# One of five wq loads issued by an ordinary, row-per-partition `dma_start`

## The chip, the cores and the metric

The kernel runs on one core of one Trainium2 chip. The metric is device microseconds of that core, the median of several executions; lower is better. A "span" is the time of one profiled execution from its first to its last instruction; it is about 1.7 us shorter than the device time of the same run.

## The reference, cut to what matters

```python
# x (1,1,640); k_cache, v_cache (1,32,32768,192); wq (640, 32*192); wo (6144, 640); all bf16
h  = x + attention(layernorm(x)) @ wo     # q = layernorm(x) @ wq; keys and values: the last 4096 positions
h2 = h + gmlp(layernorm(h))               # w_in (640,1536), w_out (768,640)
```

One token is decoded. Nearly all the work is reading: wq is 7.9 MB, the window of keys and values of 32 heads 100.7 MB, wo 7.9 MB, the gMLP weights 2.9 MB. Nothing is read twice, so the kernel is a stream of loads with arithmetic behind it.

## The kernel before

All large loads are issued on SP (the sync engine's queue) by one helper that builds the DMA instruction itself:

```python
def load(out, in_):
    eng = nc.sync
    eng.add_instruction(mybir.InstDMACopy(
        name=nc.get_next_instruction_name(), mode="Copy", queue="qSPDynamicHW",
        ins=eng.lower_ap_dma(in_, for_custom_bir_dma=True),
        outs=eng.lower_ap_dma(out, for_custom_bir_dma=True)))
...
wq_v = A_wq.rearrange("(c p i) n -> c p (i n)", c=DC, i=4)   # 5 blocks; 32 source rows of 48 KB each
...
def dma_wq(i):
    t = kvp.tile([P, KVE], BF16, tag="kv", name="wq_t")
    for c in range(2 * i, min(2 * i + 2, DC)):
        load(t[:, (c % 2) * HD:(c % 2 + 1) * HD], wq_v[c])
    tiles[("wq", i)] = t
...
plan = [("kv", lambda i=i: dma_wq(i)) for i in range(NWQ)]   # wq comes first,
...                                                          # then k, v, wo, w_in, w_out in order of use
issue()                                                      # issues until the buffers are all taken
```

Source and destination of a wq load name the same 128 x 6144 elements in the same order, but the source is described as 32 rows of 24576 elements (four rows of wq run together), the destination as 128 partitions of 6144. Three tiny loads (x, and two scalars) go out by `nc.scalar.dma_start` on ACT. The program that is built from this carries a mark, "precooked", on those three and on no load of SP: an ordinary `dma_start` gets it where the shape allows, the hand-built instruction does not.

Of the kernel before, what the change touches and what calls it, by code (L numbers as in the profile page):

```python
# [16 lines left out]
def kernel(  # L17
# [14 lines left out]
    nc = tc.nc  # L32
    P = nc.NUM_PARTITIONS
# [6 lines left out]
    HD = H * Dh  # L40
# [15 lines left out]
# [6 lines that stand above are left out]
# [11 lines left out]
    wq_v = A_wq.rearrange("(c p i) n -> c p (i n)", c=DC, i=4)  # L73
# [27 lines left out]
    def dma_wq(i):  # L101
        t = kvp.tile([P, KVE], BF16, tag="kv", name="wq_t")
        for c in range(2 * i, min(2 * i + 2, DC)):
            load(t[:, (c % 2) * HD:(c % 2 + 1) * HD], wq_v[c])
        tiles[("wq", i)] = t

    def dma_pair(kind, cache, t_):
# [6 lines left out]
    def dma_wo(q):  # L114
# [7 lines left out]
        tiles[("wo", q)] = t  # L122

    plan = [("kv", lambda i=i: dma_wq(i)) for i in range(NWQ)]
    for t_ in range(2):
        plan.append(("kv", lambda t=t_: dma_pair("k", A_k_cache, t)))
# [531 lines left out]
```

## Time and profile before

| | before |
|---|---|
| device time | 286.6 us (286.29 to 286.65, 3 runs) |
| span of the profiled run | 284.7 us |
| bytes moved, mean rate | 119.53 MB, 420 GB/s |
| large queue's packets, share of 16 engines' span | 97.8% |
| first wq issue on SP | 551 ns, from 0.74 us |
| first packet of wq | 2.073 us |
| last landing of wo_t to the end of the span | 10.6 us |

These are lines of the page of the kernel before. The first two rows have one entry for each of 40 equal slices of the span: the busy share of the 16 DMA engines in tenths (9 is 90% or more), and the rate. The last row is the queue that SP's loads run on: packets, MB, share of 16 engines' span.

```profile
DMA  8999999999998999999999999999999999999993
GB/s 332 435 435 408 435 429 402 444 463 435 435 435 382 435 442 443 427 464 424 414 442 421 443 428 439 407 457 428 410 435 456 442 442 383 435 435 425 401 406 141
DMA packets 5404, 119.53 MB, mean 420 GB/s; under 512 B 973, under 2 KB 2254, under 8 KB 2830
...
q1 hardware_dynamic: 5384, 119.35, 97.8%
```

The engines are busy from the first slice to the last but one. A 48 KB packet takes 1.815 us, so 16 engines carry 16 x 49152 B / 1.815 us = 433 GB/s. The Trainium skill, "DMA: Bandwidth & Descriptors", section "Where 436 GB/s comes from", gives 435 GB/s as the ceiling of the fabric, and this trace agrees. (The same section says that for loads from HBM the HBM side, about 358 GB/s, binds; here, with one core running, it did not: the page has 119.34 MB of HBM reads, 419 GB/s over the span.) With the engines this full, what is left to win without moving fewer bytes is the start, before the engines run, and the tail, after the last load that the end waits for.

The next lines are from the timeline of the first 12 us (start, duration, engine and line, what, and in brackets the idle time before it). SPq and ACTq are the queues that issue DMAs; an issue's duration is the sequencer's work on it, not the transfer.

```profile
0.74 3.15 SPq L58 DMA_DIRECT2D wq_t<-in_A_wq_dram  x5
...
0.91 0.50 ACTq L155 DMA_DIRECT2D x_row<-in_A_x_dram  x1
...
2.21 0.28 PE L241 MATMUL sm_ps<-ones_bf,x_row 1*128 1x1 bf16 x5 [2.21 <-DMA x_row<-in_A_x_dram]
...
6.49 0.16 DVE L245 COPY x_pc<-sm_ps 128x5 f32<-128x5 f32 x1
...
7.36 1.90 SPq L58 DMA_DIRECT2D k_t<-in_A_k_cache_dram  x3
```

Five wq issues run one after another on SP. The single records behind the first line are 551, 568, 594, 632 and 615 ns. The first ends at 1.288 us and its first packet starts at 2.073 us, so 0.785 us pass between issue and data. The k_t issue at 7.36 us waits for the first wq load to land (they share a semaphore).

The view of the wq tile tells the same by issue (min/median/max, ns), and how long each load took from issue to landing; the chain of waits shows the last load on the path and the last computation (start, duration).

```profile
L58 SPq DMA_DIRECT2D wq_t<-in_A_wq_dram x5: 551/594/632, 0.7 to 3.3; - x5
...
DMA to landing us min/median/max: 6.6/11.2/15.7
```

```profile
260.22 13.82 DMA wo_t<-in_A_wo_dram
...
281.75 0.32 DVE o_sb L629
```

The last wo_t load lands at 260.22 + 13.82 = 274.04 us. Then come 10.6 us of short dependent steps; the gMLP weights, queued behind wo, land meanwhile, and their last packet ends at 280.95 us.

### The profile page before, as it was taken

To read this page: it belongs to the slowest core of one execution; us is meant where nothing else is said; L and a number is where in the kernel's file an instruction comes from. 1 tells how busy PE (TensorE), PEld (TensorE's weight loads), DVE (VectorE), ACT (ScalarE), POOL (GpSimd) and SP (SyncE) were. 2 spreads that over 40 slices of the span, in tenths; PEclk is the share of its full clock that TensorE was granted. 3 is DMA by queue.
4 is the path that set the end of the run, shared out by engine and by line. 5 is a ranking of instruction groups with operands and counts; after the bars stand their busy time and mean duration, and the time that the engine had idled before them with its cause. 6 is when DMAs were issued, how large, how long until landed. Compare 5 with 4: busy or idle time off the path is not lost.

```text
span 284.7 us, 3101 instructions
## 1 busy us (share of the span) xinstructions
PE 167.1 (59%) x1110; PEld 65.3 (23%) x1110; DVE 218.4 (77%) x288; ACT 75.2 (26%) x380; POOL 2.3 (1%) x10
## 2 busy tenths in 40 slices
PE   0329935773755377725852585536971767764774
PEld 0103412221211022211220121112320222321463
DVE  7300099889999999998499999996699949995443
ACT  2001247413274431122344440143101010202301
POOL 3000000000000000000000000000000000000000
PEclk9999979796598557955799558955797797999785
DMA  8999999999998999999999999999999999999993
GB/s 332 435 435 408 435 429 402 444 463 435 435 435 382 435 442 443 427 464 424 414 442 421 443 428 439 407 457 428 410 435 456 442 442 383 435 435 425 401 406 141
DMA packets 5404, 119.53 MB, mean 420 GB/s; under 512 B 973, under 2 KB 2254, under 8 KB 2830
## 3 DMA queue, kind: packets, MB, share of 16 engines
q1 hardware_dynamic: 5384, 119.35, 97.8%
q8 instruction: 8, 0.13, 0.2%
q14 instruction: 6, 0.05, 0.0%
q10 hardware_dynamic: 6, 0.00, 0.0%
HBM read 119.34 MB, written 0.00 MB: 419 GB/s over the span
## 4 chain that ended last, share of the span: by engine, by line
DMA 42%; DVE 41%; PE 13%; issue 2%; SPq 1%; ACT 0%; DVEq 0%; ACTq 0%
DVE k_t L316 22%; DMA k_t<-in_A_k_cache_dram 21%; DMA v_t<-in_A_v_cache_dram 9%; DMA wq_t<-in_A_wq_dram 7%; DMA wo_t<-in_A_wo_dram 5%; PE sc_ps L264 5%; DVE S L309 5%; DVE ob L437 4%; DVE S L330 4%; PE sc_ps L323 3%; PE pv_174 L412 1%; PE attn_ps L473 1%; SPq L58 1%; PE sm_ps L340 1%; DVE gm L342 1%
## 5 line engine op out<-in xcount | busy, mean ns | idle before, releaser
L316 DVE TENSOR_TENSOR k_t<-k_t,q_205 128x6144 bf16<-128x6144 bf16 x32 | 107.1, 3351 | 13.1 <-DMA k_t<-in_A_k_cache_dram 13.1
L323 PE MATMUL sc_ps<-k_t,ident_bf 128*128 128x512 bf16 x282 | 87.1, 468 | 50.6 <-DVE k_t L316 50.6
L306 ACT ACTIVATE k_t<-k_t 128x192 bf16<-128x192 bf16 x144 | 49.9, 347 | 32.8 <-DVE k_t L316 32.8
L323 PEld LDWEIGHTS <-ident_bf 128*128 128x128 bf16 x282 | 30.6, 113 | 98.3 <-issue 63.9
L306 ACT ACTIVATION_READ_ACCUMULATOR k_t<-k_t 128x1 f32 x144 | 26.8, 186 | 0.0
L309 DVE TENSOR_REDUCE S<-k_t 128x16 f32<-128x3072 bf16 x8 | 26.8, 3345 | 0.0
L264 PE MATMUL sc_ps<-wq_t,xn_126 128*128 128x512 bf16 x60 | 17.4, 449 | 10.4 <-DMA wq_t<-in_A_wq_dram 8.1
L330 DVE TENSOR_REDUCE S<-sc_ps 128x16 f32<-128x512 f32 (+1 forms) x32 | 21.8, 682 | 0.5 <-PE sc_ps L323 0.5
L273 DVE TENSOR_SCALAR sp_f<-sm_ps 128x1 f32<-128x1 f32 x3 | 0.3, 153 | 25.3 <-PE sm_ps L270 25.3
L359 ACT ACTIVATE E_125<-S,bias 128x64 bf16<-128x64 f32 x10 | 3.5, 360 | 48.1 <-DVE bias L349 48.1
L359 ACT ACTIVATE E_123<-S,bias 128x64 bf16<-128x64 f32 x12 | 4.2, 360 | 41.9 <-DVE bias L349 41.9
L359 ACT ACTIVATE E_124<-S,bias 128x64 bf16<-128x64 f32 x10 | 3.5, 361 | 37.9 <-DVE bias L349 37.9
L266 ACT ACTIVATE q_205<-sc_ps 128x512 bf16<-128x512 f32 x6 | 3.6, 597 | 30.1 <-PE sc_ps L264 30.1
L264 PEld LDWEIGHTS <-xn_126 128*128 128x128 bf16 x60 | 6.5, 109 | 20.9 <-issue 13.6
L412 PE MATMUL pv_174<-v_t,E_124 128*8 128x512 bf16 (+1 forms) x72 | 8.9, 521 | 2.0 <-DMA v_t<-in_A_v_cache_dram 2.0
L342 DVE TENSOR_REDUCE gm<-sm_ps 2x1 f32<-2x128 f32 x16 | 4.5, 278 | 7.1 <-PE sm_ps L340 7.1
L412 PE MATMUL pv_172<-v_t,E_125 128*8 128x512 bf16 (+1 forms) x72 | 7.5, 472 | 3.1 <-DMA v_t<-in_A_v_cache_dram 3.1
L412 PE MATMUL pv_174<-v_t,E_123 128*8 128x512 bf16 (+1 forms) x48 | 5.8, 521 | 1.0 <-DMA v_t<-in_A_v_cache_dram 1.0
L412 PE MATMUL pv_172<-v_t,E_123 128*8 128x512 bf16 (+1 forms) x72 | 6.2, 424 | 0.0
L412 PE MATMUL pv_174<-v_t,E_125 128*8 128x512 bf16 (+1 forms) x48 | 5.0, 474 | 1.6 <-DMA v_t<-in_A_v_cache_dram 1.6
L412 PEld LDWEIGHTS <-E_125 128*8 128x8 bf16 (+1 forms) x120 | 3.5, 87 | 9.3 <-issue 7.2
L412 PEld LDWEIGHTS <-E_124 128*8 128x8 bf16 (+1 forms) x120 | 3.6, 89 | 8.3 <-issue 6.4
(237 smaller groups left out, 148.3 us busy)
## 6 DMA issues: line engine op xcount, KB each, us to landing
k_t<-in_A_k_cache_dram SPq DMA_DIRECT2D x15, 3072.0 KB, 29.8
v_t<-in_A_v_cache_dram SPq DMA_DIRECT2D x15, 3072.0 KB, 29.6
wq_t<-in_A_wq_dram SPq DMA_DIRECT2D x5, 1536.0 KB, 11.2
wo_t<-in_A_wo_dram SPq DMA_DIRECT2D x7, 960.0 KB, 19.9
k_t<-in_A_k_cache_dram SPq DMA_DIRECT2D x2, 1536.0 KB
v_t<-in_A_v_cache_dram SPq DMA_DIRECT2D x1, 1536.0 KB
w_in_sb<-in_B_w_in_dram SPq DMA_DIRECT2D x2, 576.0 KB, 14.6
wo_t<-in_A_wo_dram SPq DMA_DIRECT2D x2, 480.0 KB, 13.8
```

The lines of the kernel that those rows point to most:

```text
L58: eng.add_instruction(mybir.InstDMACopy(name=nc.get_next_instruction_name(), mode="Copy", queue="qSPDynamicHW", ins=eng.lower_ap_dma(in_, ...
L264: nc.tensor.matmul(psv, lhsT=xn2[:, c, a, :], rhs=wc[:, gq:gq + 4, a, w0:w0 + P], start=(c == 0 and a == 0), stop=(c == DC - 1 and a == 1))
L266: nc.scalar.activation(out=q2f[:, gq:gq + 4, w0:w0 + P], in_=psv, func=ACT.Copy, scale=scale / 16)
L306: nc.scalar.activation(out=k3[:, j, :], in_=k3[:, j, :], func=ACT.Copy, accum_out=S[:, j:j + 1])
L309: nc.vector.tensor_reduce(out=st[t]["S"][:, J - JS:J], in_=products(t)[:, J - JS:J, :], axis=AX.X, op=ALU.add)
L316: nc.vector.tensor_tensor(out=kc, in0=kc, in1=q2[:, t:t + 1, :].to_broadcast([P, JC, Dh]), op=ALU.mult)
L323: nc.tensor.matmul(psv, lhsT=ident_bf[:], rhs=products(t)[:, j0:j1, n * g:(n + 1) * g], start=(n == 0), stop=(n == Dh // g - 1))
L330: nc.vector.tensor_reduce(out=S[:, j0:j1], in_=st[t]["ps"][ch], axis=AX.X, op=ALU.add)
L342: nc.vector.tensor_reduce(out=gm[:], in_=mT[0:2, 0:P], axis=AX.X, op=ALU.max)
L359: nc.scalar.activation(out=E[:, :, a], in_=S[:], func=ACT.Exp, bias=bias[:, a:a + 1], accum_out=zq[q][:, a, b:b + 1])
L412: nc.tensor.matmul(pv[p0:p0 + 2 * n, :].rearrange("p (k r i) -> p k r i", k=n, r=32), lhsT=E[:, j0:j0 + n, :].rearrange("p j a -> p (j a)" ...
L437: nc.vector.tensor_reduce(out=ob[:, i0:i0 + ni], in_=flat.rearrange("p (k r i) -> p i r k", k=n, i=ni), axis=AX.X, op=ALU.add)
```

## The change

The intent: the first 128 rows of wq (1.5 MB) are loaded by an ordinary `dma_start` with one row of wq for each partition, which gives the instruction the mark and so the shorter issue path. It is the first large load, so nothing hides its issue.

```diff
     def dma_wq(i):
         t = kvp.tile([P, KVE], BF16, tag="kv", name="wq_t")
         for c in range(2 * i, min(2 * i + 2, DC)):
-            load(t[:, (c % 2) * HD:(c % 2 + 1) * HD], wq_v[c])
+            dst = t[:, (c % 2) * HD:(c % 2 + 1) * HD]
+            if c == 0:
+                nc.sync.dma_start(out=dst, in_=A_wq[0:P])
+            else:
+                load(dst, wq_v[c])
         tiles[("wq", i)] = t
```

It changes two things at once: the issue path (the mark), and the shape of the source (128 rows of 12 KB for 32 of 48 KB, so packets of 12 KB). No other instruction changes: of the two built programs only this one instruction differs, in the mark and in the shape of its source.

## The prediction

> **What bounds the kernel now.** The 16 DMA engines. They move 119.5 MB in a span of 284.7 us, and the big queue's packets take 97.8% of 16 engines' span (table of DMA queues). The DMA row of the 40 slices reads 9 everywhere but in the first (8) and the last (3). In the packet records, from about 2.9 to 280 us at least 16 packets are always in flight; the idle engine time before 5 us adds up to 2.34 us of all 16 engines. A 48 KB packet takes 1.815 us, so 16 engines carry 433 GB/s. The Trainium skill, "DMA: Bandwidth & Descriptors", section "Where 436 GB/s comes from", gives 435 GB/s as the ceiling; this trace agrees. The chain of waits names DVE work for much of the middle, but the DMA engines never pause there, so it does not set the time. After the last landing of wo_t (274.03 us) come some 10 us of short dependent work.
>
> So the time is: start of the stream + bytes at the ceiling + tail. Only the first is touched.
>
> **What the change does.** One of 64 DMA instructions changes: the first 1.5 MB of wq. The order of instructions is otherwise the same on every engine. The built program marks the new instruction "precooked", as it does the three small plain loads on ACT and none of the other SP loads; its source is now 128 rows of 12 KB, not 32 of 48 KB.
>
> *Removed.* In the timeline the first of the five wq issues on SP starts at 0.74 us and takes 551 ns (all: 551 to 632); its first packet starts at 2.073 us, 0.79 us after the issue ended. The three marked issues on ACT take 499, 217 and 274 ns, the first evidently cold, and x_row's first packet starts 0.41 us after its issue. My estimate: the first issue falls to 300 to 450 ns, and the data may follow a little sooner. First packet at 1.65 to 1.95 us: 0.1 to 0.4 us earlier. ACT's loads are one row each, this one 128, so it is uncertain.
>
> *Added.* 128 packets of 12 KB, 8 an engine. The trace's 64 other packets of 12 KB take 461 ns: 8 x 461 = 3.69 us against 2 x 1.815 = 3.63 us, 0.06 us lost.
>
> *Moved.* The other four wq issues go out about 0.2 us sooner, but queue behind the first. The first k_t issue (7.36 us) waits for the first wq load to land and moves with it; four wq loads are then still queued, so the engines do not starve.
>
> **On the critical path:** all of the earlier start, since the stream has no gap to swallow it. Net about 0.3 - 0.06 = 0.25 us, a tenth of a percent.
>
> **Predicted time:** 286.3 us; 285.8 to 286.7 should hold it 8 times in 10. Faster by over 2%: 0.01; within 2%: 0.98; slower by over 2%: 0.01.
>
> **What would show each step.** The first wq issue under 480 ns; the first big packet before 2.0 us; 128 more packets of 12 KB at about 461 ns and 32 fewer of 48 KB; the DMA row at 9 from the second slice to the 39th; every wq_t landing and the last wo_t landing earlier by the same 0.1 to 0.4 us; the span after it unchanged.
>
> **What would make it wrong.** The first precooked issue on SP may be as cold as ACT's (499 ns), leaving little. All engines' first packets are slow in the trace (2.06 to 2.68 us against 1.815); four times as many may take longer to get going and eat the gain. The scatter of runs (286.29 to 286.65) is as large as the effect. A changed order of packets could open a gap at a later buffer hand-over.

## The result, and the profile after

The changed kernel takes 286.1 us (median of 6 runs, 285.96 to 286.27), beside 286.55 us for the kernel before (6 runs, 286.29 to 286.89). The ratio is 0.9984 with a 95% interval of 0.9971 to 0.9997.

The page after, the same lines:

```profile
DMA  8999999999999999999999999999999999999993
GB/s 332 443 443 443 415 409 430 428 446 436 443 443 410 422 415 444 428 471 431 415 436 422 430 436 439 418 453 422 424 422 457 443 443 384 436 436 418 405 406 145
DMA packets 5500, 119.53 MB, mean 421 GB/s; under 512 B 973, under 2 KB 2254, under 8 KB 2830
...
q1 hardware_dynamic: 5480, 119.35, 97.8%
```

There are 96 more packets (128 of 12 KB for 32 of 48 KB) and the same bytes; the stream is as full as before.

The timeline of the first 12 us after:

```profile
0.73 0.38 SPq L106 DMA_DIRECT2D wq_t<-in_A_wq_dram  x1
...
0.91 0.50 ACTq L159 DMA_DIRECT2D x_row<-in_A_x_dram  x1
...
1.18 2.88 SPq L58 DMA_DIRECT2D wq_t<-in_A_wq_dram  x4
...
3.91 0.29 PE L245 MATMUL sm_ps<-ones_bf,x_row 1*128 1x1 bf16 x5 [3.91 <-DMA x_row<-in_A_x_dram]
...
6.48 0.16 DVE L249 COPY x_pc<-sm_ps 128x5 f32<-128x5 f32 x1
6.86 1.86 SPq L58 DMA_DIRECT2D k_t<-in_A_k_cache_dram  x3
```

The first issue takes 380 ns, not 551. Its first packet starts at 1.740 us, 0.333 us earlier: 0.171 us of that is the shorter issue, the rest is that the data now follow the end of the issue after 0.627 us, not 0.785. The k_t issue, which waits for this load to land, comes 0.50 us earlier (this size does not repeat: 6.86 us here, but 7.34 and 7.36 us in the kept traces of the same kernel, e1 and e9, beside 7.36 and 7.67 us for before and its repeat e5). One thing got later: x_row's load of 1280 bytes now apparently finds wq packets in front of it; its packet starts at 3.019 us and not at 1.818, and PE's first matmul comes at 3.91 us and not at 2.21. That costs nothing: DVE is busy with its constants until it reads the result at 6.48 us, as before.

The wq tile's view, and the end of the chain of waits:

```profile
L58 SPq DMA_DIRECT2D wq_t<-in_A_wq_dram x4: 541/596/1022, 1.2 to 3.5; - x4
L106 SPq DMA_DIRECT2D wq_t<-in_A_wq_dram x1: 380/380/380, 0.7 to 0.7; - x1
...
DMA to landing us min/median/max: 6.1/10.8/14.9
```

```profile
259.82 13.82 DMA wo_t<-in_A_wo_dram
...
281.33 0.32 DVE o_sb L633
```

The last wo_t load lands at 259.82 + 13.82 = 273.64 us, 0.40 us earlier than before; the rest of the span is again 10.6 us. In this pair of profiles what was won at the start is there at the end; how exactly it is passed on is the matter of the experiments. (The third wq issue on SP, at 1.76 us, now takes 1022 ns; two loads, over 7 us of transfer, were issued before it, and nothing waits for it.)

### The profile page after: what moved, and what is told of

It reads as the page before. It is cut to its first block, busy times and chain, and to the rows that moved or that the text cites. A ratio compares the mean times of both kernels' runs of the same rounds, so it can differ in the third digit from the quotient of the medians.

```text
span 284.3 us, 3101 instructions
## 1 busy us (share of the span) xinstructions
PE 167.4 (59%) x1110; PEld 65.5 (23%) x1110; DVE 218.2 (77%) x288; ACT 75.2 (26%) x380; POOL 2.3 (1%) x10
## 4 chain that ended last, share of the span: by engine, by line
DMA 42%; DVE 40%; PE 13%; issue 2%; SPq 1%; ACT 0%; DVEq 0%; ACTq 0%
DVE k_t L320 22%; DMA k_t<-in_A_k_cache_dram 21%; DMA v_t<-in_A_v_cache_dram 9%; DMA wq_t<-in_A_wq_dram 6%; DMA wo_t<-in_A_wo_dram 5%; PE sc_ps L268 5%; DVE S L313 5%; DVE ob L441 4%; DVE S L334 4%; PE sc_ps L327 3%; PE attn_ps L477 1%; SPq L58 1%; PE pv_174 L416 1%; PE sm_ps L344 1%; DVE gm L346 1%
## 5 line engine op out<-in xcount | busy, mean ns | idle before, releaser
L327 PE MATMUL sc_ps<-k_t,ident_bf 128*128 128x512 bf16 x282 | 88.0, 471 | 52.5 <-DVE k_t L320 52.5
L416 PE MATMUL pv_172<-v_t,E_125 128*8 128x512 bf16 (+1 forms) x72 | 8.2, 500 | 3.1 <-DMA v_t<-in_A_v_cache_dram 3.1
L416 PE MATMUL pv_174<-v_t,E_124 128*8 128x512 bf16 (+1 forms) x72 | 8.0, 488 | 1.9 <-DMA v_t<-in_A_v_cache_dram 1.9
L416 PE MATMUL pv_172<-v_t,E_123 128*8 128x512 bf16 (+1 forms) x72 | 6.2, 424 | 0.0
L416 PE MATMUL pv_174<-v_t,E_123 128*8 128x512 bf16 (+1 forms) x48 | 5.3, 490 | 1.3 <-DMA v_t<-in_A_v_cache_dram 1.3
L416 PE MATMUL pv_174<-v_t,E_125 128*8 128x512 bf16 (+1 forms) x48 | 5.0, 472 | 1.7 <-DMA v_t<-in_A_v_cache_dram 1.7
```

What stands on the lines that cost most here:

```text
L327: nc.tensor.matmul(psv, lhsT=ident_bf[:], rhs=products(t)[:, j0:j1, n * g:(n + 1) * g], start=(n == 0), stop=(n == Dh // g - 1))
L416: nc.tensor.matmul(pv[p0:p0 + 2 * n, :].rearrange("p (k r i) -> p k r i", k=n, r=32), lhsT=E[:, j0:j0 + n, :].rearrange("p j a -> p (j a)" ...
```

## The experiments

The theory, T: the stream of loads has no gap, so an earlier first packet moves the end by as much, and the earlier packet comes from the marked issue path. The rivals: R, the smaller packets make the gain; S, the start is swallowed later and the gain is elsewhere; and that it is scatter, since the effect is no larger than the spread of runs.

Because the effect is so small, each run was read in two ways. The times are medians beside the kernel before in the same set. And from the packet records of each trace I took, for the loads' packets of 512 bytes and more: the start of the first one; the *missing engine time* before 10 us, that is the sum over time of (16 minus packets in flight)/16, taken as 0 where more than 16 are in flight; and the end of the last one.

| run | what | first packet, us | missing, us | end of stream, us | end minus missing, us | span, us | median, us (before in that set) |
|---|---|---|---|---|---|---|---|
| before | unmarked | 2.07 | 2.35 | 280.95 | 278.60 | 284.66 | 286.55 |
| after | marked | 1.74 | 2.17 | 280.56 | 278.39 | 284.25 | 286.10 (286.55) |
| e1 | marked (after again) | 1.74 | 2.30 | 280.82 | 278.52 | 284.66 | 286.55 (286.81) |
| e2 | rows, unmarked | 2.09 | 2.59 | 281.05 | 278.46 | 284.86 | 286.70 (286.81) |
| e3 | last wq marked | 2.09 | 2.55 | 281.23 | 278.68 | 284.92 | 286.73 (286.81) |
| e4 | after + 1 tiny load ahead | 2.10 | 2.48 | 281.01 | 278.53 | 284.86 | 286.82 (286.81) |
| e5 | unmarked (before again) | 2.10 | 2.66 | 281.23 | 278.57 | 285.07 | 286.59 (286.82) |
| e6 | after + 3 tiny loads ahead | 2.74 | 3.03 | 281.76 | 278.73 | 285.98 | 287.65 (286.82) |
| e7 | first load in 5, marked | 1.75 | 3.13 | 282.16 | 279.02 | 287.08 | 288.21 (286.82) |
| e8 | first load in 5, unmarked | 2.09 | 4.28 | 283.03 | 278.75 | 286.97 | 288.88 (286.82) |
| e9 | marked (after again) | 1.75 | 2.31 | 280.91 | 278.60 | 284.76 | 286.50 (286.77) |
| e10 | first load 16 + 112 rows, marked | 1.76 | 1.97 | 282.82 | 280.85 | 286.91 | 288.85 (286.77) |
| e11 | first load 64 + 64 rows, unmarked | 2.10 | 2.23 | 284.26 | 282.03 | 288.07 | 289.82 (286.77) |
| e12 | all five wq by rows, marked | 1.76 | 2.20 | 280.75 | 278.55 | 284.57 | 286.37 (286.77) |

In the e1 set both that kernel and before have strays (287.7 to 287.9 us), so means and ratios are wider there than medians. The sets are before and after; e1 to e4; e5 to e8; e9 to e12. The kernels of one set ran on the same chip.

The kept traces of e1 to e4 are of other executions than those behind their rows and lines here. They are second profiles: first packet 1.76, 2.08, 2.09 and 2.10 us; missing 2.12, 2.47, 2.55 and 2.59; end minus missing 278.80, 278.98, 278.76 and 278.63; span 284.60, 285.28, 284.99 and 285.99.

One more reading of the fourteen kept traces shows where time is lost. Spread each packet's bytes evenly over its duration, and note when the large queue has moved 8 MB (a little more than wq) and when 110 MB. From the first to the second takes 236.2 to 236.4 us in every run, whatever happened at the start: a late start is passed on whole up to there. The 8 MB are reached at 21.11 to 21.37 us with a marked first load of 128 rows (after, e1, e9, e12) and at 21.41 to 21.72 us with an unmarked one (before, e2, e3, e5). The means are 0.34 us apart, as the first packets are; across the sets the gap between the groups is only 0.04 us, but within a set the difference is 0.30 (after against before) and 0.37 to 0.39 us (e1 against e2 and e3). The others: e4 21.62, e6 22.23, e7 22.63, e8 23.63, e10 23.27, e11 24.73 us.

### e1: the changed kernel again

No edit. Expected:

> The changed kernel once more, as the control of this set. Theory (T): the stream of loads is never idle once begun, so an earlier first packet moves the end by as much. First wq issue about 380 ns, first packet at about 1.74 us, span about 284.3 us, ratio to before 0.9985. If the gain of the first measurement was scatter: ratio 1.000 and a span of 284.6.

Measured: first issue 392 ns, first packet at 1.74 us, median 286.55 us beside 286.81. The span is 284.66 us where 284.3 was expected: this set ran about 0.26 us slower, before included. The ratio is 0.9998 (0.9976 to 1.0019), because two strays lie in the mean of six. By ratio and span alone e1 came out where the expectation had put scatter (1.000 and 284.6), so the timing does not settle it here; the first packet repeats to two hundredths of a microsecond (1.74, and 1.76 in the second profile).

### e2: the shape of the change without the mark

```diff
             if c == 0:
-                nc.sync.dma_start(out=dst, in_=A_wq[0:P])
+                load(dst, A_wq[0:P])
```

> Only half of the change: the source in 128 rows of 12 KB, but by the unmarked issue path. T (the issue path makes the gain): first issue 550 ns, first packet at about 2.07 us, span 284.6 to 284.8, ratio 1.000 to 1.0005. Rival R (the smaller packets make the gain, because the engines get under way sooner with small ones and no engine waits for a 48 KB packet to end): first packet still at about 2.07 us, but the first load lands earlier by 0.3 us or more and the span is 284.3 to 284.4, ratio 0.9985. If both share: first packet about 1.9 us, span 284.45.

Measured: the first packet comes at 2.09 us and the missing time is 2.59 us; both are those of the unmarked kernels (2.07 to 2.10, and 2.35 to 2.66). The wq issues, in the wq tile's view of e2:

```profile
L58 SPq DMA_DIRECT2D wq_t<-in_A_wq_dram x5: 576/593/597, 0.7 to 3.3; - x5
```

The median is 286.70 us, 0.15 us over e1 and 0.11 under before. So R falls: small packets alone start nothing earlier. The built programs of e2 and of the changed kernel differ in one field, the mark on this one load, so nothing else in the program can make the difference at the start. The gap of 0.78 us between issue and data (0.735 + 0.576 = 1.311 to 2.09 us) is also there, so the shorter gap belongs to the mark too, not to the shape.

### e3: the last wq load marked, not the first

```diff
-            if c == 0:
-                nc.sync.dma_start(out=dst, in_=A_wq[0:P])
+            if c == DC - 1:
+                nc.sync.dma_start(out=dst, in_=A_wq[c * P:(c + 1) * P])
```

> The same edit on the last of the five wq loads instead of the first. T: its issue falls from about 615 to about 350 ns, but four loads are queued before it, so nothing follows; its 12 KB packets cost 0.06 us. Span 284.6 to 284.8, ratio 1.0000 to 1.0005. Rival R (small packets help as such): span 284.3, ratio 0.9985.

Measured: start and end of the stream are those of an unmarked kernel (2.09 us; 281.23 us), median 286.73 beside 286.81 us. So 12 KB packets bring nothing here either, against R. But the expectation for the issue missed: it took 588 ns, not about 350, although the built program has the mark on it.

```profile
L106 SPq DMA_DIRECT2D wq_t<-in_A_wq_dram x1: 588/588/588, 3.2 to 3.2; - x1
```

With no shorter issue, e3 does not test whether a shorter one is worth nothing behind other loads; e12 does. In e12 marked issues that follow one another took 394, 413, 432, 692 and 445 ns. Why a marked issue behind four unmarked ones is slow was not tried, so "the mark saves 0.17 us wherever it stands" is not shown.

### e4 and e6: delaying the changed kernel's first load

```diff
+    for i in range(1):     # e6: range(3)
+        nc.sync.dma_start(out=const.tile([1, 2], BF16, name=f"dly{i}")[:, 0:1], in_=B_b_sp.rearrange("(o n) -> o n", o=1))
     issue()
```

> The changed kernel with one 2-byte load issued on SP ahead of the first wq load, which delays it. T: the dummy's issue is 0.25 to 0.4 us (plus 0.06 between), the first packet comes at 2.0 to 2.2 us, and the span grows against e1_after_again by the same amount as the first packet moved, within 0.1 us: 284.5 to 284.7, ratio 0.9995 to 1.0005. Rival S (the start is swallowed by later slack and the gain lies elsewhere, e.g. in the earlier k_t issue or in the PE's start): first packet later, span unchanged at 284.3.

> The changed kernel with three 2-byte loads issued on SP ahead of the first wq load (e4 had one). T: each costs about 0.40 us of SP's time (e4: 336 ns and 59 ns between), so the first packet of wq comes at about 2.95 us, 1.2 us later than in e1, and the span grows by 1.1 to 1.3 us against e1: 285.6 to 286.1, ratio to before 1.002 to 1.004. Rival S (later slack swallows the start): span 284.7 as in e1, ratio 1.000.

The timeline of SP in e4, then in e6:

```profile
0.73 0.34 SPq L156 DMA_DIRECT2D dly<-in_B_b_sp_dram  x1
1.13 0.36 SPq L106 DMA_DIRECT2D wq_t<-in_A_wq_dram  x1
```

```profile
0.73 0.90 SPq L156 DMA_DIRECT2D dly<-in_B_b_sp_dram  x3
1.67 0.37 SPq L106 DMA_DIRECT2D wq_t<-in_A_wq_dram  x1
```

Against e1, the first packet moved by 0.36 us in e4 and by 1.00 us in e6; the end of the stream by 0.19 and 0.94 us; the median, each taken over before in its own set, by 0.27 and 1.09 us (e4: +0.01 against -0.26; e6: +0.83 against -0.26). The tiny loads cost less than expected once the first was out (215 and 243 ns), so e6's first packet moved less than the expected 1.2 us; its span grew by 1.32 us, because the steps after the stream took longer too. In e4 the span grew by 0.20 us where the first packet moved by 0.36: the expected agreement within 0.1 us missed, and its ratio of 1.0011 lies above the expected 1.0005, with two strays in the mean. In e4 one tiny load takes back about the gain of the change. S falls by e6, where the delay is clear of the scatter: a later start is a later end. (e6 ran on another chip than e1, so its ends are less comparable than its medians.)

### e5: the kernel before, as a kernel of its own

> The kernel before, as a kernel of its own: a second profile of it, because the first set ran on a chip on which every kernel took about 0.25 us more, and because the 16 engines' first packets are spread differently in every profile. Theory T: first wq issue about 550 ns, first packet at 2.05 to 2.1 us, span 284.6 to 285.1, ratio 1.000 with an interval that shows what the timing can resolve (about 0.002). If the start differs by 0.2 us or more from the first profile of this kernel, the profiles can't carry the comparison.

Measured: first packet at 2.10 us, missing time 2.66 us, span 285.07 us: unmarked, as before. The missing time of the same kernel thus differs by 0.31 us between two profiles, more than the 0.2 us that the expectation allowed; only the first packet repeats (2.07 and 2.10). And its ratio to the very same kernel is 0.9984 (0.9967 to 1.0002), the number that the change got, with medians of 286.59 and 286.82 us. So a median of six runs resolves no better than about 0.2 us here, and no single timing proves a gain of 0.3. The evidence is in the traces: the first packet comes at 1.74 to 1.76 us in every profile of a kernel with a marked first load of 128 rows and nothing ahead of it, and at 2.07 to 2.10 in every profile with an unmarked one. The missing time is weaker evidence: in four profiles of kernels with a marked first load of 128 rows (after, e1, e9, e12) the missing time is 2.17 to 2.31 us, in four with an unmarked one (before, e2, e3, e5) 2.35 to 2.66, with no overlap but only 0.04 us between (the second profiles of e1 to e3 fall within these bounds or outside them on their own side); and the three differences of medians between the changed kernel and before all have one sign: 0.45, 0.26 and 0.27 us, while the same kernel twice gave 0.23.

The missing time varies within one kernel because the 16 engines do not start together. In before the first packets spread from 2.07 to 2.90 us, in e3 from 2.09 to 3.64, in after from 1.74 to 2.48. What sets that spread was not found.

### e7 and e8: five issues at the start, marked and unmarked

```diff
-                nc.sync.dma_start(out=dst, in_=A_wq[0:P])
+                for a, b in ((0, 256), (256, 512), (512, 768), (768, 1024), (1024, HD)):
+                    nc.sync.dma_start(out=dst[:, a:b], in_=A_wq[0:P, a:b])   # e7; e8: load(dst[:, a:b], A_wq[0:P, a:b])
```

> The first wq load in five loads of the marked path: four of 256 columns (64 KB each, 0.15 us of transfer) and the rest. Issue-bound at the start. T: five issues of 360 to 390 ns plus 60 between, the rest's first packet at about 3.2 us; the four small ones fill 0.6 us of that; span 0.8 to 1.0 us over e1 (285.4 to 285.8), ratio 1.002 to 1.003.

> The same five loads by the unmarked path. T: five issues of 560 to 600 ns plus 60 between, the rest's first packet at about 4.5 us, 1.1 to 1.3 us later than in e7, and the span longer than e7's by the same 1.1 to 1.3 us (286.5 to 287.0), ratio 1.006 to 1.008. Rival R (the shape of the packets is what counts, the path is not): the same as e7.

Here the cost of the issues is multiplied until it stands clear of the scatter: same loads, same packets; the built programs differ in the mark on the five issues alone. The wq tile's view of e7 (its five cut loads), then of e8 (all nine of wq):

```profile
L107 SPq DMA_DIRECT2D wq_t<-in_A_wq_dram x5: 388/432/432, 0.7 to 2.6; - x5
```

```profile
L58 SPq DMA_DIRECT2D wq_t<-in_A_wq_dram x9: 575/593/602, 0.7 to 5.8; - x9
```

A marked issue is about 0.16 us shorter (432 for 593 ns in the medians), much as in the change itself (0.171). The missing time differs by 1.15 us, as expected (1.1 to 1.3); the end of the stream differs by 0.87 us, the medians by 0.67 us (288.21 and 288.88), less than expected. e8 came out where it was expected (ratio 1.0064, span 286.97 us). e7 did not: its missing time is 0.83 us over e1's, as foreseen, but its stream ends 1.34 us later and its median, taken over before in its set, is 1.65 us higher (+1.39 against -0.26). Its profiled run is a stray besides (288.8 us, 0.6 over its own median), so its span says little (it is even 0.11 us longer than e8's, against the expectation). The kept traces show where e7's extra half microsecond went: the first packet of the rest came at 3.66 us, not at the expected 3.2, and e7 is 1.30 us behind e1's kept trace when 8 MB have moved and 1.27 us behind at 110 MB. So it was lost in the first loads, not later; a packet in flight counts as full in the missing time, however slowly it moves (the 512-byte packets took 27 ns, which is 16 x 512 B / 27 ns = 303 GB/s). In the same measure e8 is 1.00 us behind e7, with its rest's first packet 1.01 us later (4.67 us). What is settled is the sign and the rough size of the mark's effect where nothing else differs: R, which had the two equal, falls again.

### e9: control for the last set

No edit.

> The changed kernel a third time, beside the kernel before, as control for the next three. Theory T: first wq issue about 385 ns, first packet at 1.74 us, missing engine time before 10 us 2.1 to 2.35 us (the profiles with an unmarked first load: 2.35, 2.55, 2.59, 2.66), median time 0.2 to 0.45 us under that of before. If the gain was scatter: the same median as before.

Measured as T expects: first issue 395 ns, first packet at 1.75 us, missing time 2.31 us, median 286.50 us beside 286.77 (ratio 0.9995, 0.9982 to 1.0008).

### e10 and e11: trying to beat the change by cutting the first load by rows

```diff
-                nc.sync.dma_start(out=dst, in_=A_wq[0:P])
+                for a, b in ((0, 16), (16, P)):     # e11: ((0, 64), (64, P))
+                    nc.sync.dma_start(out=dst[a:b], in_=A_wq[a:b])
```

> The changed kernel with its first load cut by rows: 16 rows (one for each engine), then 112, both marked. Tries to beat the change. T: an issue of one row took 336 ns cold and 215 to 243 ns warm (e4, e6), one of 128 rows 380 to 392 ns, so 16 rows should take about 345 ns and the first packets come at about 1.70 us, with the 16 engines less spread; the second issue ends at about 1.5 us, its packets come at about 2.15 us, just as the first end. Missing engine time before 10 us 1.9 to 2.2 us, time 0 to 0.2 us under e9. If the second issue comes too late, a gap of 0.2 to 0.4 us opens and it is slower than e9 by that.

> The same, cut into 64 and 64 rows: whether the length of the first issue goes with its rows. T: about 360 ns, first packet at about 1.72 us, no gap (the first half is 1.8 us of transfer); missing engine time and time as e9 within 0.1 us.

Both are slower by 2 to 3 us: 288.85 us (ratio 1.0075) and 289.82 us (1.0109). The start of e10 was in part as hoped: the least missing time of all (1.97 us), but the issue of 16 rows took 393 ns, not 345, and the first packet came at 1.76 us, not 1.70. The transfer was not as hoped. The stretches from 4 to 6 and from 6 to 8 us (busy time of the engines, granted clock, DMA share, GB/s) in e9, e11 and e10:

```profile
4.00:6.00 2.00, 0.29 (x5) 0.21 (x5) 1.86 (x21) 0.00 (x0) 0.00 (x0) 1.00 1.05 436
6.00:8.00 2.00, 0.60 (x2) 0.50 (x2) 1.17 (x8) 0.00 (x0) 0.00 (x0) 1.00 1.30 559
```

```profile
4.00:6.00 2.00, 0.00 (x0) 0.00 (x0) 1.86 (x21) 0.00 (x0) 0.00 (x0) 1.00 0.96 203
6.00:8.00 2.00, 0.60 (x2) 0.50 (x2) 1.17 (x8) 0.00 (x0) 0.00 (x0) 1.00 0.93 197
```

```profile
4.00:6.00 2.00, 0.28 (x5) 0.20 (x5) 1.86 (x21) 0.00 (x0) 0.00 (x0) 1.00 0.97 276
6.00:8.00 2.00, 0.60 (x2) 0.50 (x2) 1.18 (x8) 0.00 (x0) 0.00 (x0) 1.00 1.12 326
```

The last number is what counts (a 48 KB packet's bytes are booked where it starts, so 559 is not a real rate). With 64 partitions at a time the 16 engines are all busy (a share of 0.93 to 0.96) and move about 200 GB/s; many of e11's 12 KB packets take about 960 ns, against 460 in e9. The Trainium skill, "SBUF — State Buffer", section "Door 1: The DMA port swizzle", gives a reason: partitions 0 to 63 reach only 8 of the 16 ports through which DMA writes the memory, for which it gives about 218 GB/s. This trace agrees roughly, with 197 to 203; the ports themselves no run here shows. For e10, whose 112 rows give every engine 7, the like (engines that share ports) is a likely cause but was only argued.

e11 says nothing about what it was made for. The build does not mark a load of 64 rows, so its issues took 590 and 571 ns; its expectation rests on a mark that is not there. Unplanned, it shows that an ordinary `dma_start` without the mark is as slow to issue as the hand-built load.

### e12: all five wq loads by rows and marked

```diff
-            if c == 0:
-                nc.sync.dma_start(out=dst, in_=A_wq[0:P])
+            if c < DC:
+                nc.sync.dma_start(out=dst, in_=A_wq[c * P:(c + 1) * P])
```

> All five wq loads by rows and marked. T: only the first one's issue is on the path; the other four are queued while the engines are busy, so their shorter issues bring nothing, and their 12 KB packets cost 4 x 0.06 us = 0.24 us of stream. First packet at 1.74 us, time 0.1 to 0.3 us over e9, so about as the kernel before. Rival (shorter issues are worth something anywhere): 0.2 us or more under e9.

The wq issues of e12:

```profile
L106 SPq DMA_DIRECT2D wq_t<-in_A_wq_dram x5: 394/432/692, 0.7 to 2.9; - x5
```

Measured: median 286.37 us beside 286.50 for e9 and 286.77 for before; end of the stream 280.75 us, 0.16 before e9's, of which 0.11 is missing time. The expected loss of 0.24 us is not seen, and a gain of 0.13 is below what the medians resolve. The four later issues took 1.98 us together, against 2.80 in e9, yet 8 MB had moved at 21.35 us against 21.37: the 0.82 us saved behind other loads bought nothing that shows. The loss had been worked out from packet durations (461 ns against 1815/4 = 454). Durations overlap a little: the spacing of starts on the 16 engines is 458 ns for 12 KB packets in after and 1812 ns for 48 KB ones in before, so 458 against 453, 0.04 us for a load and about 0.15 for four. (A rougher check: from 3 to 8 MB moved takes 11.63 us in e12 and 11.54 in e9.) Whether e12 beats the change is open.

## Why the prediction was right

- *The bound.* Right. End of stream minus missing time at the start is 278.4 to 278.7 us in ten of the fourteen profiles, whatever was done at the start, as long as the packets flow at the ceiling. The clear exceptions are e10 and e11, whose loads did not. e8 and e7 (278.75 and 279.02 us) lie hardly further out than the second profiles (278.63 to 278.98), so this difference is good to some 0.6 us. The firmer evidence is the 236.2 to 236.4 us from 8 to 110 MB in all fourteen traces. One detail was misread: the DMA row before has an 8 in the 13th slice too, which is no gap: by the packet records only 0.06 us of all 16 engines' time is missing there (a packet's share is booked where it starts).
- *The issue.* Predicted 300 to 450 ns, measured 380 (392 and 395 in the repeats). Marked issues on ACT had served as the model (499, 217 and 274 ns), and the range was wide enough for most of what lies between them.
- *The first packet.* Predicted at 1.65 to 1.95 us, best guess 1.8; measured 1.74. The guess that "the data may follow a little sooner" was right and worth nearly half of it (0.158 of 0.333 us). The prediction gave no reason for it beyond x_row's 0.41 us, and e2 shows that it comes with the mark; so hitting the sum was in part luck.
- *The packets.* 128 more of 12 KB and 32 fewer of 48 KB, with a median of 461 ns, as predicted. The price of 0.06 us was too high: 0.04 us by the spacing of packets, and not seen in any median.
- *Passing it on.* Right. The last wo_t landing came 0.40 us earlier, the tail after it stayed at 10.6 us; and e6 shows that a delay at the start is passed on too. The five wq landings came 0.50 to 0.56 us earlier, more than the foretold 0.1 to 0.4. Such sizes do not repeat: e9's wq loads land within 0.1 us of before's (another set and chip), while e1's kept trace is 0.30 to 0.34 us ahead of e5.
- *The size.* Predicted 0.25 us net and 286.3 us, measured 286.1 us; the three differences of medians are 0.45, 0.26 and 0.27 us. The term that was a little too small is the first packet's (0.27 us guessed, 0.333 measured), and 0.06 us for the packets was too much to take off. That 286.1 us lies in the predicted range (285.8 to 286.7) proves little, since the unchanged kernel's 286.55 us lies in it too; what bears the prediction out is the chain of events, issue, first packet and the time of 8 MB. The rest of the 0.40 us at the last landing is within the scatter of the missing time from profile to profile, and the same kernel twice differed by 0.23 us in time (e5). The stated fear that scatter is as large as the effect was justified.

## What to carry to other kernels

When the DMA engines are full from end to end, what a change of issues can win is before the first packet; there, 0.3 us sooner is about 0.3 us of run time (clear of scatter only where the delay was made larger, in e6 and e8), while shorter issues of loads that queue behind others bought nothing that showed (e12). Judge an effect of a tenth of a percent by the event it should move (here the first packet and the time at which 8 MB have moved), in several profiles and with the unchanged kernel run as its own control, because the timings alone gave the same ratio for the unchanged kernel. Leave an early load whole rather than cut it by partitions: a load of fewer than 128 partitions may run at a fraction of the rate although all 16 engines are busy.

## What the Trainium skill lacked or had wrong

- No page tells of the marked issue path. "DMA: Bandwidth & Descriptors" gives no issue time for trn2's hardware path by shape: here an unmarked issue of a wq load on SP mostly took 541 to 632 ns (the third wq load of after, e1 and e9 947 to 1031), a marked one 380 to 395 at the start and 362 to 445 behind other marked ones (692 once) but 588 behind four unmarked ones, a marked one of 16 rows 393, and a marked one of one row 215 to 243 after a first of 332.
- The same page, section "Latency and other measured facts", gives about 600 ns to the first byte. It does not say from where it counts. Measured from the end of the issue, the marked load agrees (0.627 us); the unmarked one needed 0.785 us.
- The same page, section "Issuing engines are not separate DMA queues", calls the issue time "usually small relative to the DMA itself". So it is (0.38 to 0.55 us for a load of 3.6 us), but at the first load of a full stream it still shows: 0.33 us at the first packet, 0.17 of it from the issue itself.
- The same page, section "Rules for kernel authors", advises for the use of all 16 engines an outermost dimension that is a multiple of 16, "ideally the 128 partitions". The runs bear out the second half: 64 and 112 rows are multiples of 16, kept the engines busy, and ran at 197 to 203 and 276 to 326 GB/s. "SBUF — State Buffer" has a reason and a number for 64; no page has a number for 112.
- No page says how far apart the 16 engines start on one load: 0.7 to 1.6 us between the first and the last in the profiles with a first load of 128 partitions in one piece.
